# Repeating the pooled-attention means with one fp16 product instead of an fp32 one, with the stage table re-timed

## The chip, the cores and the metric

The kernel runs on one core of a Trainium2 chip. A core has five engines that work side by side, each through its own list of instructions in order: TensorE (PE, matrix products into PSUM), VectorE (DVE), ScalarE (ACT), GpSimd (POOL) and SyncE (SP, which here only issues DMAs). They wait for each other by semaphores. The metric is device time in microseconds (us), and lower is better.

## The reference

The reference is an attention block whose output goes through a mixture of experts. Only the first part is touched here. B = 8 batches, H = 8 heads, S = 576 tokens, D = 64:

```python
q_d = q.reshape(B, H, Sd, factor, D).mean(axis=3)
k_d = k.reshape(B, H, Sd, factor, D).mean(axis=3)
v_d = v.reshape(B, H, Sd, factor, D).mean(axis=3)
out_d = sm_attn(q_d, k_d, v_d)
out_up = np.repeat(out_d, factor, axis=2)
mask = np.abs(pos[:, None] - pos[None, :]) < factor
scores = np.where(mask, scale * np.matmul(q, k.transpose(0, 1, 3, 2)), -1000000000.0)
...
return (out_up + out_local).astype(np.float32)
```

`sm_attn` is softmax attention, here among 144 means of four tokens each; each mean's result then stands for its 4 tokens. `out_local` is softmax attention of each token over the 7 tokens around it.

The sum, laid out as 4608 tokens by 512 values (x), is then routed: gate scores x @ w_gate, a greedy assignment with a capacity of 576 tokens per expert, and for each of 8 experts relu(x @ w1) @ w2 on its own tokens.

## The kernel before

The work has three stages, one after the other. Attention makes x and the gate scores; routing picks an expert and its tokens; the experts' products follow, with later routing beside them.

Attention walks over 36 **units** of 128 tokens (4 windows of 32), 4.5 units to a batch. Batch work (transposing q and k, summing groups of four, attention among the 144 means) is spread between the units. A unit's steps on PE are: `loc_s` (scores, L485 and L494), `loc_t` (four transposes, L514), `loc_v` (32 small products, L536), `rows` (L475, repeats the means), `log_t` (four transposes of x, L554), `log_m` (gate products, L569 and L572). Between them stand, on DVE, the maximum and subtraction after `loc_s` (L503, L504), the `norm` after each half of `loc_v` (L439, L440, L442), the addition of the repeated means (`log_a`, L544), and the low half of x (L559); and, on ACT, the exponential (L506), the copies of the transposed scores (`pt`, L525) and the high half of x (L558).

A batch's means come from `down_v` (L398, L403, L411). Its `end()` normalizes them into `u32`, fp32, 128 means by 512, with DVE. The last 16 of the 144 means, the tail, are spread by POOL into `ut32` (L429). `rows(u)` then makes 128 token rows out of 32 rows of means with a product whose weights `rep` are zeros and ones; a unit that runs over the end of a batch's first 128 means uses two products of 64 rows, one of them with `rept` and `ut32`. This holds for the first 27 units, those of batches 0 to 5 (`ADDU`); for the last nine the means go through DRAM (`UPB` = 6).

The order is written by hand. `run` gives each step a time in units: unit number plus the step's entry in `LOC`, or a place in a spread (`TW`, `DW`) for batch work, or an entry in `NEXT` for a load; it sorts the steps by that time and records them in that order, and each engine runs its own instructions in the order recorded. Steps that use PE are **pieces**; `after(n, f)` records f only n pieces later, and `need(key)` records it at once. `FN`, `FL`, `FT`, `FD` are such distances. `EV` is a cycle that says which copies out of PSUM go to DVE (1) and which to ACT (0). Products write to PSUM tiles named g, of which there are six (`NG`), and one tile named s for the scores.

```python
LOC = {'up': 1.7, 'um': 4.3, 'st': 4.6, 't': 1.3, 'lm': 8.07, 's0': 0.33, 's1': 0.331, 'lt': 5.61, 'v0': 1.83, 'v1': 1.831, 'add': 4.5}
```

Of the kernel before, what the change touches and what calls it, by code (L numbers as in the profile page):

```python
# [6 lines left out]
F32 = mybir.dt.float32  # L7
# [26 lines left out]
GSN = ()  # L34
SH1 = 0.6
EARLY = 1
# [3 lines left out]
LT = 5  # L40
NEXT = (("q0", 1.3), ("q1", 1.6), ("k0", 1.9), ("k1", 2.2), ("t", 2.6), ("q2", 2.9), ("q3", 3.2), ("k2", 3.5), ("k3", 3.8),
        ("v0", 4.1), ("v1", 4.4), ("v2", 4.7), ("v3", 5.0), ("w", 5.2))
VWS = 0.25
PACE0 = 0.6
FD = 4
FN = 2
FL = 3
FT = 2
PEL = ("s0", "s1", "t", "v0", "v1", "lt", "lm")
TW = (0.23, 2.44)  # L50
DW = (0.15, 1.9)
DWS = {0: (1.96, 3.4), 7: (0.82, 2.25)}
LOC = {'up': 1.7, 'um': 4.3, 'st': 4.6, 't': 1.3, 'lm': 8.07, 's0': 0.33, 's1': 0.331, 'lt': 5.61, 'v0': 1.83, 'v1': 1.831, 'add': 4.5}
GS1 = ''
# [8 lines left out]
PEV = (0,0)  # L63
EV = (0,0,0,0,0,1)
UPB = 6
# [4 lines left out]
GS = 32.0  # L70
VWT = 1.75
T0 = (-0.12, 0.19)
LD0 = (-1.79, -1.53, -1.57, -0.7, 0.51)
LD1 = (-0.99, -0.95, -0.9, -0.89, -0.88, -0.6, -0.55, -0.3, -0.25, 0.2, 0.4, 0.6, 0.8, 2.0)
TWS = {1: (1.4, 2.75)}
E0 = 0.54
E1 = 0.55
# [17 lines left out]
class Attention:  # L95
    def __init__(self, ctx, tc, q, k, v, wg, ident, identb, maskc, x_dram, up_dram, lg, big, more=()):
# [14 lines left out]
        self.ident, ident = ident  # L111
        identh = cst.tile([128, 130 + H + GT + QW], BF, name="identb")
        self.identb, self.half, self.own8 = identh[:, :128], identh[:, 128:130], identh[:, 130:130 + H]
        self.own16, self.eye = identh[:, 130 + H:130 + H + GT], identh[:, 130 + H + GT:]
        self.wm = cst.tile([128, 128], BF, name="wm")
# [10 lines left out]
        for i in range(2):  # L126
# [5 lines left out]
            self.vd.append(cst.tile([128, 2, H, D + 1], F32, name=f"vd{i}"))  # L132
        self.rep = cst.tile([128, 4 * 128], F32, name="rep")
        self.rept = cst.tile([128, 4 * GT], F32, name="rept")
        self.u32 = [cst.tile([128, H, D], F32, name=f"u32{i}") for i in range(2)]
        self.ut32 = [cst.tile([128, H, D], F32, name=f"ut32{i}") for i in range(2)]
        for i in range(4):
# [12 lines left out]
    def fixed(self, part):  # L150
# [17 lines left out]
        else:  # L168
# [4 lines left out]
            for t in self.vw[2:]:  # L173
                nc.gpsimd.memset(t, 1.0)
            nc.scalar.copy(self.rep.rearrange("p (g f) -> p g f", f=4), self.identb[:, :, None].to_broadcast([128, 128, 4]))
            nc.scalar.copy(self.rept.rearrange("p (g f) -> p g f", f=4), self.own16[:, :, None].to_broadcast([128, GT, 4]))
            heads(nc.gpsimd, nc.gpsimd, self.qdz[1])
# [213 lines left out]
    def down_v(self, b, g):  # L391
# [21 lines left out]
        def end():  # L413
            x = self.u32[b % 2][:, 4 * g:4 * g + 4]
            r = self.norm(o, x, 4 + g, 4.0)
            if b >= UPB:
                up = self.up_dram[b * G:b * G + 128, 256 * g:256 * g + 256]
                nc.sync.dma_start(up, x.rearrange("p h d -> p (h d)"))
            if g:
                own = self.wk.tile([128, 2], F32, name="own")  # L420
                nc.vector.tensor_tensor(own, r[:, 4:].to_broadcast([128, 2]), self.half, op=OP.mult)
                y = self.wk.tile([128, D], F32, name="yu")
                nc.vector.tensor_scalar(y, o[:, 260:324], own[:, :1], None, op0=OP.mult)
                nc.vector.scalar_tensor_tensor(y, o[:, 325:389], own[:, 1:], y, op0=OP.mult, op1=OP.add)
                if b >= UPB:
                    nc.sync.dma_start(bass.AP(tensor=up.tensor, offset=up.offset - 256 * g + 128 * HD,
                                              ap=[[D, H], [HD, 16], [1, D]]), y)
                else:
                    nc.gpsimd.tensor_tensor(self.ut32[b % 2], y[:, None].to_broadcast([128, H, D]),  # L429
                                            self.own8[:, :, None].to_broadcast([128, H, D]), op=OP.mult)  # L430

        self.after(FN, end, ("v", b, g))

    def norm(self, o, dst, m, n):
# [8 lines left out]
        return r  # L443

    def load_up(self, u):
        for b in {4 * u // NW, (4 * u + 3) // NW}:
            for g in range(2):
                self.need(("v", b, g))
        if u < ADDU:
# [10 lines left out]
    def rows(self, u):  # L460
# [6 lines left out]
        for r0 in (0, 64):  # L467
            b, l = divmod(32 * u + r0 // 4, G)
            t = (self.u32 if l < 128 else self.ut32)[b % 2].rearrange("p h d -> p (h d)")
            parts.append((r0, 64, self.rep[:, 4 * l:4 * l + 64] if l < 128 else self.rept, t, (b, l < 128), l))  # L470
        if parts[0][4] == parts[1][4]:
            l = parts[0][5]
            parts = [(0, 128, self.rep[:, 4 * l:4 * l + 128], parts[0][3])]
        for r0, n, w, t, *_ in parts:
            nc.tensor.matmul(o[r0:r0 + n], w, t, start=True, stop=True)  # L475
        self.up[u] = o
# [880 lines left out]
def _constants():  # L1357
# [11 lines left out]
    for (_, step), (n, nxt) in zip(LV, LV[1:] + ((1, 0),)):  # L1369
# [7 lines left out]
        "ident": np.eye(128, dtype=np.float32),  # L1377
        "identb": np.concatenate([np.eye(128), p[:, None] // 16 % 2 == np.arange(2), p[:, None] // GT == np.arange(H), p[:, None] % GT == np.arange(GT), p[:, None] % 64 == np.arange(QW)], 1).astype(np.float32).astype(bf),
        "mask": m.transpose(2, 0, 1, 3).reshape(128, 4, 4 * KW).astype(bf),
# [29 lines left out]
```

## Time and profile before

| what | value |
|---|---|
| time, median of 3 runs | 741.86 us (738.19 to 743.55) |
| profiled execution, its own time | 735.96 us |
| span of that execution, first to last instruction | 734.1 us |
| busy, whole span: PE / DVE / ACT / POOL | 91% / 72% / 45% / 31% |
| mean granted TensorE clock | 0.964 |

The profile is of one execution, which took 5.9 us less than the median of the three runs. Times in it count from the start of the span. Attention fills some 40 us of start, a steady part from 40 to 240 us, and its last units until about 275 us; the first routing follows until 305 us, and the experts the rest.

### The profile page before, as it was taken

How to read it: one execution, taken by the hardware profiler on the slowest of the kernel's cores; microseconds unless marked ns; L12 is line 12 of the kernel's file. 1: busy time of each engine (PE TensorE's matmuls, PEld its weight loads, DVE VectorE, ACT ScalarE, POOL GpSimd, SP SyncE). 2: the span in 40 equal slices, each digit the busy share in tenths (PEclk: the TensorE clock that was granted, in tenths of full speed). 3: DMA queues.
4: the chain of work that ended last, by engine and by line, in shares of the span. 5: the costliest groups of instructions: out<-in, count | busy, mean ns of one | idle time of the engine just before them, and what ended most of it. 6: DMA issues, size and time to landing. Idle time of an engine off the chain costs nothing.

```text
span 734.1 us, 21924 instructions
## 1 busy us (share of the span) xinstructions
PE 671.5 (91%) x8919; PEld 454.4 (62%) x8919; DVE 527.0 (72%) x1575; ACT 334.0 (45%) x637; POOL 227.3 (31%) x296
## 2 busy tenths in 40 slices
PE   7889998999999872699999899999999999999994
PEld 4677777677777661475575375475575574664751
DVE  5687686778777887897889698798797796534500
ACT  4566657586776430451542443443444334434410
POOL 4766172625626440300601501302204104401011
PEclk9799999999999985799999999999999999999998
DMA  9998959788896650712706706717627439905001
GB/s 267 219 201 225 232 135 244 204 194 202 200 225 171 153 173 12 239 57 93 266 2 232 171 23 255 162 28 267 138 85 242 98 141 234 343 2 122 9 29 37
DMA packets 142356, 116.21 MB, mean 158 GB/s; under 512 B 91440, under 2 KB 120112, under 8 KB 142256
## 3 DMA queue, kind: packets, MB, share of 16 engines
q1 hardware_dynamic: 134960, 93.27, 47.8%
q0 software_dynamic: 6432, 20.98, 9.0%
q8 instruction: 71, 1.16, 0.7%
q10 hardware_dynamic: 864, 0.56, 0.3%
q14 instruction: 29, 0.24, 0.1%
HBM read 88.23 MB, written 19.46 MB: 147 GB/s over the span
## 4 chain that ended last, share of the span: by engine, by line
PE 52%; DVE 17%; issue 15%; ACT 6%; DMA 6%; POOL 2%; SPq 0%; POOLq 0%; ACTq 0%; DVEq 0%
PE pX L1243 13%; PE pH L1202 12%; PE g L536 5%; PE g L475 3%; PE g L318 3%; DVE wl L1126 2%; PE s L494 2%; PE g L554 2%; PE g L514 2%; PE pR L799 2%; DVE ht L1229 2%; DVE level L766 2%; DMA nat<-in_moe_w_dram 1%; POOL out_dram L1253 1%; PE g L398 1%
## 5 line engine op out<-in xcount | busy, mean ns | idle before, releaser
L1202 PE MATMUL pH<-xt,wh 128*128 128x256 f16 (+1 forms) x1024 | 194.7, 286 | 1.6 <-DVE xt L1163 0.8
L1243 PE MATMUL pX<-wh,ht 128*128 128x512 f16 (+1 forms) x640 | 177.9, 380 | 0.0
L1202 PE MATMUL pH<-xt,wl 128*128 128x320 f16 (+1 forms) x512 | 146.2, 286 | 0.0
L1243 PEld LDWEIGHTS <-ht 128*128 128x128 f16 (+1 forms) x960 | 82.1, 100 | 94.6 <-issue 5.4
L1243 PE MATMUL pX<-wl,ht 128*128 128x512 f16 (+1 forms) x320 | 117.6, 380 | 0.0
L1202 PEld LDWEIGHTS <-wh 128*128 128x128 f16 x1024 | 98.0, 98 | 29.3 <-issue 6.3
L1126 DVE SCALAR_TENSOR_TENSOR wl<-nat,wh 128x512 f16<-128x512 f32 x128 | 83.5, 687 | 25.0 <-ACT wh L1124 22.0
L1253 POOL DMA_INDIRECT out_dram<-y,idx x40 | 43.4, 1086 | 181.9 <-ACT y L1250 158.9
L1226 ACT ACTIVATE ht<-pH 128x512 f16<-128x512 f32 (+1 forms) x128 | 45.5, 407 | 114.7 <-PE pH L1202 114.7
L1250 ACT ACTIVATE y<-pX 128x512 f32<-128x512 f32 (+1 forms) x40 | 23.8, 595 | 108.9 <-PE pX L1243 61.4
L1124 ACT ACTIVATE wh<-nat 128x1024 f16<-128x1024 f32 x64 | 67.4, 1053 | 8.7 <-DMA nat<-in_moe_w_dram 8.7
L1229 DVE SCALAR_TENSOR_TENSOR ht<-pH,ht 128x512 f16<-128x512 f32 (+1 forms) x128 | 52.3, 450 | 26.2 <-ACT ht L1226 25.7
L1141 POOL DMA_INDIRECT xg<-x_dram,idx x40 | 42.9, 1071 | 64.8 <-DVE cl L1026 45.5
L1202 PEld LDWEIGHTS <-wl 128*128 128x128 f16 x512 | 50.0, 98 | 13.5 <-issue 1.7
L525 ACT COPY pt<-g 64x512 f32<-64x512 f32 x72 | 41.7, 579 | 33.3 <-PE g L514 31.8
L536 PE MATMUL g<-vw,pt 128*64 128x65 f32 x1152 | 45.9, 230 | 2.7 <-ACT pt L525 2.4
L536 PEld LDWEIGHTS g<-vw,pt 128*64 128x64 f32 x1152 | 40.5, 143 | 9.7 <-ACT pt L525 6.0
L304 ACT COPY qt<-g 64x512 f32<-64x512 f32 (+1 forms) x50 | 31.4, 628 | 32.4 <-PE g L318 19.1
L318 PE MATMUL g<-ident,nat 128*128 128x128 f32 x256 | 41.1, 286 | 3.8 <-DMA nat<-in_q_dram 2.3
L304 ACT COPY kt<-g 64x512 f32<-64x512 f32 (+1 forms) x60 | 37.9, 631 | 9.2 <-PE g L318 8.5
L291 POOL TENSOR_TENSOR gtmp<-kt 128x576 f32<-128x576 f32 x14 | 16.0, 1146 | 78.6 <-ACT kt L304 68.3
L949 POOL MEMSET f<- 128x1 bf16 x8 | 0.9, 109 | 118.7 <-DVE s L888 52.8
(219 smaller groups left out, 1143.7 us busy)
## 6 DMA issues: line engine op xcount, KB each, us to landing
nat<-in_moe_w_dram SPq DMA_DIRECT2D x28, 1024.0 KB
vw<-in_v_dram SPq DMA_DIRECT2D x136, 96.0 KB
x_dram<-x SPq DMA_DIRECT2D x36, 256.0 KB
nat<-in_q_dram SPq DMA_DIRECT2D x32, 256.0 KB
nat<-in_k_dram SPq DMA_DIRECT2D x32, 256.0 KB
nat<-in_v_dram SPq DMA_DIRECT2D x28, 256.0 KB
up<-up_dram SPq DMA_DIRECT2D x9, 256.0 KB
nat<-in_moe_w_dram SPq DMA_DIRECT2D x4, 512.0 KB
```

The source lines that it names most:

```text
L304: self.nc.scalar.copy(out, in_)
L318: nc.tensor.transpose(p[:, a, :, fp], src[:, 4 * hh + 2 * a + s, 2 * fp:2 * fp + 2].rearrange("p f d -> p (f d)"), self.ident)
L525: self.nc.scalar.copy(out, in_)
L536: nc.tensor.matmul(o[64 * i:64 * i + 64, 65 * h:65 * h + 65], pt[:, 2 * (h % 2) + i, 2 * g + h // 2].rearrange("p b q -> p (b q)"), self.v ...
L1124: nc.scalar.activation(hi, r, AF.Copy, scale=sc)
L1126: nc.vector.scalar_tensor_tensor(lo[:, a:a + LOP], r[:, a:a + LOP], sc, hi[:, a:a + LOP], op0=OP.mult, op1=OP.subtract)
L1141: self.fetched = nc.gpsimd.indirect_dma_start(out=xg[:n], out_offset=None, in_=self.x, in_offset=bass.IndirectOffsetOnAxis(ap=idx[:n, c:c ...
L1202: mm = nc.tensor.matmul(p[:, s, :s1 - s0], w[d][a][:, 128 * f:128 * f + 128], xt[:, b, d, s0:s1], start=j == 0, stop=j == len(seq) - 1)
L1226: last = nc.scalar.activation(hi, q, AF.Relu)
L1229: low = nc.vector.scalar_tensor_tensor(lo, q, 0.0, hi, op0=OP.max, op1=OP.subtract)
L1243: mm = nc.tensor.matmul(p[o:o + m], ht[:, f, h0:h0 + m], w[4 + f // 2][b][:, 512 * (f % 2):512 * (f % 2) + 512], start=j < parts, stop=j > ...
L1253: i = nc.gpsimd.indirect_dma_start(out=self.out, in_=y[:n], in_offset=None, out_offset=bass.IndirectOffsetOnAxis(ap=idx[:n, c:c + 1], axis=0))
```

## The change

The normalized means are kept as a pair of fp16 numbers, high and low, each scaled by 32 (`XS`). For means 0 to 63 the high half lies on partitions 0 to 63 and the low half on 64 to 127 of `u16[:, 0]`; for means 64 to 127, `u16[:, 1]` has the high half on 64 to 127 and the low one on 0 to 63. A product over 128 partitions with weights that are 1/32 in row j and row j + 64 then adds the two halves and repeats the mean. `rep` is fp16 and covers 64 means; `rept` is fp16. A unit whose 32 means cross from the first 64 to the next uses two products of 64 rows; a tail uses two products, one with the high and one with the low half.

`end()` writes its fp32 result to a work tile `xu`; `highs` makes the high halves on ACT (four of 64x256 and one of 128x64 for a batch), and `lows`, recorded `FH` pieces later, the low halves on DVE, and spreads the tail on POOL twice. `load_up` sees to it that all is recorded before the first unit that needs it. Batches 6 and 7 keep the way through DRAM. The table of times is also changed: `rows`, `loc_t`, `loc_v`, `log_t`, loads of the next batch, loads of v, distances in pieces, and one copy in five instead of six goes to DVE.

```diff
-SH1 = 0.6
+SH1 = 0.4
-NEXT = (("q0", 1.3), ("q1", 1.6), ("k0", 1.9), ("k1", 2.2), ("t", 2.6), ("q2", 2.9), ("q3", 3.2), ("k2", 3.5), ("k3", 3.8),
-        ("v0", 4.1), ("v1", 4.4), ("v2", 4.7), ("v3", 5.0), ("w", 5.2))
-VWS = 0.25
+NEXT = (("q0", 1.46), ("q1", 1.76), ("k0", 2.06), ("k1", 2.37), ("t", 2.77), ("q2", 3.07), ("q3", 3.38), ("k2", 3.68), ("k3", 3.98),
+        ("v0", 4.28), ("v1", 4.59), ("v2", 4.89), ("v3", 5.19), ("w", 5.4))
+VWS = 0.26
-FN = 2
+FN = 1
+FH = 2
-FT = 2
+FT = 3
-LOC = {'up': 1.7, 'um': 4.3, 'st': 4.6, 't': 1.3, 'lm': 8.07, 's0': 0.33, 's1': 0.331, 'lt': 5.61, 'v0': 1.83, 'v1': 1.831, 'add': 4.5}
+LOC = {'up': 2.07, 'um': 4.35, 'st': 4.6, 't': 1.194, 'lm': 8.07, 's0': 0.33, 's1': 0.331, 'lt': 5.483, 'v0': 1.842, 'v1': 1.843, 'add': 4.5}
-EV = (0,0,0,0,0,1)
+EV = (0, 0, 0, 0, 1)
-VWT = 1.75
+VWT = 1.24
-E0 = 0.54
+E0 = 0.72
...
-        self.rep = cst.tile([128, 4 * 128], F32, name="rep")
-        self.rept = cst.tile([128, 4 * GT], F32, name="rept")
-        self.u32 = [cst.tile([128, H, D], F32, name=f"u32{i}") for i in range(2)]
-        self.ut32 = [cst.tile([128, H, D], F32, name=f"ut32{i}") for i in range(2)]
+        self.rep = cst.tile([128, 4 * 64], F16, name="rep")
+        self.rept = cst.tile([128, 4 * GT], F16, name="rept")
+        self.u16 = [cst.tile([128, 2, H, D], F16, name=f"u16{i}") for i in range(2)]
+        self.ut16 = [cst.tile([128, 2, H, D], F16, name=f"ut16{i}") for i in range(2)]
...
-            x = self.u32[b % 2][:, 4 * g:4 * g + 4]
+            x = self.wk.tile([128, 4, D], F32, name="xu")
...
-                else:
-                    nc.gpsimd.tensor_tensor(self.ut32[b % 2], y[:, None].to_broadcast([128, H, D]),
-                                            self.own8[:, :, None].to_broadcast([128, H, D]), op=OP.mult)
+            if b < UPB:
+                self.after(FH, lambda: self.highs(b, g, x, y), ("h", b, g))
...
+    def highs(self, b, g, x, y):
+
+        nc = self.nc
+        us = []
+        for i in range(2):
+            hi, lo = slice(64 * i, 64 * i + 64), slice(64 - 64 * i, 128 - 64 * i)
+            u16 = self.u16[b % 2][:, i, 4 * g:4 * g + 4]
+            us.append((u16[lo], x[hi], u16[hi]))
+        if g:
+            yh = self.wk.tile([128, 2, D], F16, name="yh", bufs=1)
+            us.append((yh[:, 1], y, yh[:, 0]))
+        for lo, x, hi in us:
+            nc.scalar.activation(hi, x, AF.Copy, scale=XS)
+
+        def lows():
+            for lo, x, hi in us:
+                nc.vector.scalar_tensor_tensor(lo, x, XS, hi, op0=OP.mult, op1=OP.subtract)
+            if g:
+                for i in range(2):
+                    nc.gpsimd.tensor_tensor(self.ut16[b % 2][:, i], yh[:, i, None].to_broadcast([128, H, D]),
+                                            self.own8[:, :, None].to_broadcast([128, H, D]), op=OP.mult)
+
+        self.after(FH, lows, ("l", b, g))
...
-            t = (self.u32 if l < 128 else self.ut32)[b % 2].rearrange("p h d -> p (h d)")
-            parts.append((r0, 64, self.rep[:, 4 * l:4 * l + 64] if l < 128 else self.rept, t, (b, l < 128), l))
+            if l < GM:
+                t, w = (self.u16[b % 2][:, l // 64],), self.rep[:, 4 * (l % 64):4 * (l % 64) + 64]
+            else:
+                t, w = (self.ut16[b % 2][:, 0], self.ut16[b % 2][:, 1]), self.rept
+            parts.append((r0, 64, w, t, (b, l // 64), l))
...
-        for r0, n, w, t, *_ in parts:
-            nc.tensor.matmul(o[r0:r0 + n], w, t, start=True, stop=True)
+        for r0, n, w, ts, *_ in parts:
+            for i, t in enumerate(ts):
+                nc.tensor.matmul(o[r0:r0 + n], w, t.rearrange("p h d -> p (h d)"), start=i == 0, stop=i == len(ts) - 1)
```

The change moves instructions on three engines. Line numbers of the changed kernel are some 30 higher. First PE, at a unit that repeats means of batch 3: here `rows` (writing g from u and rep) stands between `log_m` (reading xt) and `loc_t` (reading sw) before.

```order
L572 MATMUL g<-wg_118,xt 128x8
L318 MATMUL g<-ident,nat 128x128 x4
L475 MATMUL g<-u_136,rep 128x512
L514 MATMUL g<-ident,sw_144 128x128 x4
L485 LDWEIGHTS identb
```

In the changed kernel the same step stands behind `loc_s` (reading kt and qt) and ahead of `log_t` (reading x) and `loc_v` (reading vw and pt); the rows are of a unit without batch work.

```order
L526 MATMUL s<-kt,qt 32x38 x32
L507 LDWEIGHTS rep
L507 MATMUL g<-u_136,rep 128x512
L586 MATMUL g<-ident,x 128x128 x4
L568 MATMUL g<-vw_142,pt_146 64x65 x16
L601 LDWEIGHTS xt
```

So `rows` now lies between `loc_t` and `loc_v`, and no longer between `loc_s` and `loc_t`. Next DVE behind the `down_v` of batch 4 in the changed kernel: u is the fp16 pair, yh that of the tail, xu the fp32 means, and mx and sw belong to the next unit's scores.

```order
L442 TENSOR_SCALAR den<-g 128x4
L443 RECIPROCAL den<-den 128x4
L445 TENSOR_TENSOR x<-g,den 128x256
L464 SCALAR_TENSOR_TENSOR u_135<-xu,u_135 64x256 x4
L464 SCALAR_TENSOR_TENSOR yh<-yu,yh 128x64
L606 TENSOR_REDUCE lg<-g 128x8
L305 COPY kt<-g 64x2x256 x2
L535 TENSOR_REDUCE mx<-s 128x8
L536 TENSOR_TENSOR sw_143<-s,mx 128x8x38
```

The five low halves have been put ahead of the maximum and subtraction of the next scores. Last ACT in the changed kernel, at the same place.

```order
L538 ACTIVATE sw_144<-sw_144 128x8x38
L307 COPY kt<-g 64x2x256 x2
L460 ACTIVATE u_135<-xu 64x256 x4
L460 ACTIVATE yh<-yu 128x64
L307 COPY qt<-g 64x2x256 x2
L557 COPY pt_146<-g 64x16x32 x2
```

The five high halves stand between copies of the next batch's k and q and ahead of the copies `pt`.

## Rows read from the trace of the kernel before

**Rows 1.** By stretch: length; busy of PE, PEld, DVE, ACT, POOL; clock; DMA share; GB/s.

```profile
40.00:240.00 200.00, 191.03 (x4507) 148.22 (x4503) 151.40 (x434) 135.31 (x268) 101.76 (x148) 0.99 0.83 204
240.00:275.00 35.00, 27.45 (x686) 22.96 (x685) 29.28 (x91) 15.40 (x32) 13.87 (x17) 0.90 0.57 160
275.00:305.00 30.00, 12.71 (x129) 8.35 (x126) 23.76 (x98) 6.08 (x8) 3.99 (x6) 0.54 0.30 95
```

**Rows 2.** Waits in 40 to 240 us: total us, times, longest.

```profile
DVE mx L503 <- PE s L494: 25.1, 22, 2.9
DVE den L439 <- PE g L536: 10.9, 10, 3.0
...
PE g L536 <- ACT pt L525: 1.9, 4, 0.5
```

**Rows 3.** Chain that ended last, 128 to 150 us: start, length, what.

```profile
129.04 0.86 PE g L475 x2
...
131.06 0.77 issue
...
139.16 1.01 PE g L475 x4
```

**Rows 4.** Groups by line and shape, L475.

```profile
L475 PE MATMUL g<-u,rep 128*128 128x512 f32 x42 | 22.0, 605 | 0.0
```

**Rows 5.** Timeline of PE in the experts' stage, fp16 products of 512 columns.

```profile
345.50 0.38 PE L1243 MATMUL pX<-wl,ht 128*128 128x512 f16 x1
345.72 0.59 PE L1243 MATMUL pX<-wh,ht 128*128 128x512 f16 x2
346.15 0.38 PE L1243 MATMUL pX<-wl,ht 128*128 128x512 f16 x1
```

**Rows 6.** Groups by line and shape: operations like the added ones.

```profile
L302 DVE COPY qt<-g 64x512 f32<-64x512 f32 x20 | 13.8, 689 | 5.9 <-PE g L318 5.3 <-PE s L494 0.3 <-ACT ptd L304 0.2
L559 DVE SCALAR_TENSOR_TENSOR xt<-g,xt 128x512 f16<-128x512 f32 x36 | 24.6, 684 | 4.9 <-ACT xt L558 4.9
L1229 DVE SCALAR_TENSOR_TENSOR ht<-pH,ht 128x64 f16<-128x64 f32 x64 | 13.6, 213 | 0.0
L1169 ACT ACTIVATE xs<-xg 128x512 f16<-128x512 f32 x24 | 14.8, 627 | 14.6 <-DMA xg<-x_dram,idx 12.9 <-DVE pi L1037 0.9 <-DVE xs L1170 0.7
L1226 ACT ACTIVATE ht<-pH 128x64 f16<-128x64 f32 x64 | 13.9, 218 | 0.0
L429 POOL TENSOR_TENSOR ut<-yu,identb 128x512 f32<-128x512 f32 x6 | 6.3, 1044 | 16.5 <-DVE den L439 16.5
```

**Rows 7.** Busy time in 5 us stretches, first and last with DVE over 4.5.

```profile
40.00:45.00 5.00, 4.50 (x170) 3.89 (x167) 4.54 (x21) 1.62 (x3) 4.61 (x9) 1.00 1.02 205
...
235.00:240.00 5.00, 4.95 (x145) 4.28 (x144) 4.61 (x13) 2.77 (x6) 4.61 (x7) 1.00 0.98 251
```

**Rows 8.** Timeline of DVE; idle time and its releaser in brackets.

```profile
137.24 0.47 DVE L503 TENSOR_REDUCE mx<-s 128x8 f32<-128x304 f32 x1 [1.34 <-PE s L494]
...
165.61 0.47 DVE L503 TENSOR_REDUCE mx<-s 128x8 f32<-128x304 f32 x1 [0.69 <-PE s L494]
```

**Rows 9.** Timeline of ACT at the same places.

```profile
138.32 0.46 ACT L506 ACTIVATE sw<-sw 128x304 f32<-128x304 f32 x1
...
162.85 1.25 ACT L304 COPY qt<-g 64x512 f32<-64x512 f32 x2 [1.97 <-PE g L318]
164.13 1.26 ACT L304 COPY kt<-g 64x512 f32<-64x512 f32 x2
```

**Rows 10.** Timeline of PE: its longest wait in the steady part.

```profile
83.58 1.36 PE L331 MATMUL g<-ident,natt 128*64 128x128 f32 x14 [1.83 <-issue]
```

**Rows 11.** Busy time in 1 us stretches behind that wait.

```profile
84.00:85.00 1.00, 1.00 (x12) 0.67 (x8) 0.00 (x0) 0.00 (x0) 0.00 (x0) 0.57 1.09 326
85.00:86.00 1.00, 1.00 (x9) 0.67 (x11) 0.00 (x0) 0.97 (x3) 0.00 (x0) 0.50 1.17 272
87.00:88.00 1.00, 1.00 (x17) 0.89 (x14) 0.88 (x5) 0.15 (x1) 0.00 (x0) 0.73 1.11 223
```

More of the change, by code (lines that the diff above doesn't have):

```diff
@@ L111, in __init__ @@
         self.ident, ident = ident
-        identh = cst.tile([128, 130 + H + GT + QW], BF, name="identb")
+        identh = cst.tile([128, 194 + H + GT + QW], BF, name="identb")
         self.identb, self.half, self.own8 = identh[:, :128], identh[:, 128:130], identh[:, 130:130 + H]
-        self.own16, self.eye = identh[:, 130 + H:130 + H + GT], identh[:, 130 + H + GT:]
+        self.own16, self.eye = identh[:, 130 + H:130 + H + GT], identh[:, 130 + H + GT:130 + H + GT + QW]
+        self.own64 = identh[:, 130 + H + GT + QW:]
         self.wm = cst.tile([128, 128], BF, name="wm")
@@ L174, in fixed @@
                 nc.gpsimd.memset(t, 1.0)
-            nc.scalar.copy(self.rep.rearrange("p (g f) -> p g f", f=4), self.identb[:, :, None].to_broadcast([128, 128, 4]))
-            nc.scalar.copy(self.rept.rearrange("p (g f) -> p g f", f=4), self.own16[:, :, None].to_broadcast([128, GT, 4]))
+            for t, i, n in ((self.rep, self.own64, 64), (self.rept, self.own16, GT)):
+                nc.scalar.activation(t.rearrange("p (g f) -> p g f", f=4), i[:, :, None].to_broadcast([128, n, 4]),
+                                     AF.Copy, scale=1.0 / XS)
             heads(nc.gpsimd, nc.gpsimd, self.qdz[1])
@@ L418, in end @@
                 nc.sync.dma_start(up, x.rearrange("p h d -> p (h d)"))
+            y = None
             if g:
@@ L447, in load_up @@
             for g in range(2):
-                self.need(("v", b, g))
+                for n in "vhl":
+                    self.need((n, b, g))
         if u < ADDU:
@@ L468, in rows @@
             b, l = divmod(32 * u + r0 // 4, G)
-            t = (self.u32 if l < 128 else self.ut32)[b % 2].rearrange("p h d -> p (h d)")
-            parts.append((r0, 64, self.rep[:, 4 * l:4 * l + 64] if l < 128 else self.rept, t, (b, l < 128), l))
+            if l < GM:
[3 more added lines that the diff above has]
+            parts.append((r0, 64, w, t, (b, l // 64), l))
         if parts[0][4] == parts[1][4]:
-            l = parts[0][5]
+            l = parts[0][5] % 64
             parts = [(0, 128, self.rep[:, 4 * l:4 * l + 128], parts[0][3])]
-        for r0, n, w, t, *_ in parts:
-            nc.tensor.matmul(o[r0:r0 + n], w, t, start=True, stop=True)
+        for r0, n, w, ts, *_ in parts:
+            for i, t in enumerate(ts):
+                nc.tensor.matmul(o[r0:r0 + n], w, t.rearrange("p h d -> p (h d)"), start=i == 0, stop=i == len(ts) - 1)
         self.up[u] = o
@@ L1377, in _constants @@
         "ident": np.eye(128, dtype=np.float32),
-        "identb": np.concatenate([np.eye(128), p[:, None] // 16 % 2 == np.arange(2), p[:, None] // GT == np.arange(H), p[:, None] % GT == np.arange(GT), p[:, None] % 64 == np.arange(QW)], 1).astype(np.float32).astype(bf),
+        "identb": np.concatenate([np.eye(128), p[:, None] // 16 % 2 == np.arange(2), p[:, None] // GT == np.arange(H), p[:, None] % GT == np.arange(GT), p[:, None] % 64 == np.arange(QW), p[:, None] % 64 == np.arange(64)], 1).astype(np.float32).astype(bf),
         "mask": m.transpose(2, 0, 1, 3).reshape(128, 4, 4 * KW).astype(bf),
```

## Prediction

> **What bounds the kernel now.** I read the busy times by stretch first. From 40 to 240 us PE is busy 191.0 of 200 us, DVE 151.4, ACT 135.3 and POOL 101.8, and the DMA share is 0.83 [rows 1]; in the two stretches behind, DVE is the busiest engine, and the clock falls to 0.54 in the second. So PE bounds the steady part, and every product with `rep` lies in it. The waits say the same from the other side: DVE stands still for PE's scores 25.1 us in 22 places and for `loc_v` 10.9 us in 10, while PE's wait for an ACT copy is 1.9 us in all [rows 2]. The chain that ended last has `rows` in it at each unit, 0.86 us for a full unit and 1.01 for one with a tail [rows 3]. What is taken from PE there shortens the kernel, as long as DVE, the next fullest, follows.
>
> **The change part by part.** *PE's products, removed.* The trace shows each fp32 product of 512 columns as two instructions: 42 for the 21 units with one product of 128 rows [rows 4]. In the chain a full one costs 0.86 us. An fp16 product of 512 columns costs 0.65 / 3 = 0.216 us: in the experts' stage three of them fill the time from 345.50 to 346.15 [rows 5]. After the change 18 units have one fp16 product: 18 x (0.86 - 0.216) = 11.6 us. Three units cross from mean 63 to 64 and have two of 64 rows: between 0.22 us, if they run side by side as the two fp32 halves of a tail did (1.01 us for four instructions that would need 1.72 in a row), and 0.43, one after the other; taken 0.33: 3 x 0.53 = 1.6. Six units with a tail have three products, 0.43 to 0.65 us, taken 0.54: 6 x 0.47 = 2.8. Sum **16.0 us** off PE, bounds 15.0 to 17.
>
> *The halves, added.* Per batch, for six batches, ACT makes four of 64x256 and one of 128x64, DVE the same number. The trace has 512 and 64 columns: on DVE 684 and 213 ns, on ACT 627 and 218 [rows 6]. On the line between them 256 columns cost 0.415 and 0.393 us. DVE: 24 x 0.415 + 6 x 0.213 = 11.2 us; ACT: 24 x 0.393 + 6 x 0.218 = 10.7 us. POOL gets 6 x 1.04 = 6.3 us, on an engine that is half empty; nothing reads its result for more than a unit, so nothing. The new `EV` moves two pairs of copies and one single from ACT to DVE by the recorded order: 4 x 0.689 [rows 6], and 0.4 for half as many columns, = 3.2 us. DVE then has 151.4 + 14.4 = 165.8 us of work in about 184, that is 90%; ACT 142.8, 78%; PE 175, 95%.
>
> *What DVE cannot give.* Two terms. (a) In 7 of the 40 stretches of 5 us DVE is busy over 4.5 us [rows 7]; where it is full, PE's saving turns into waiting: 16.0 x 7 / 40 = 2.8 us, and the same share of the moved copies, 0.6. (b) The five low halves stand ahead of the next scores' maximum: 4 x 0.415 + 0.213 = 1.87 us. At such a place DVE had 0.69 us idle ahead of that maximum (165.61) [rows 8], so the maximum is 1.2 us late. Behind it PE wants the exponential for `loc_t`: maximum at 137.24, exponential ended at 138.78 [rows 8, 9], 1.54 us. PE used to have `log_t`, `loc_v`, `log_m` and `rows` in between, and now has the first three, about 2.1 us: some 0.5 us to spare. So 0.7 us of waiting per batch, 6 x 0.7 = 4.2 us; bounds 0 (ACT's and PE's other work moves with it) and 6 x 1.87 = 11.2 us.
>
> *The order of steps.* `rows` moves from between `loc_s` and `loc_t` to between `loc_t` and `loc_v`. What it costs is in (b); what it gives is time for the copies `pt`, the 1.9 us that PE waited for [rows 2]: -1.9 us, bounds 0 and -1.9. The loads of the next batch come some 0.16 units later and v's windows half a unit later, on SP's queue, which nothing else of the steady part waits behind but the stores of x; the windows are still asked for three units before `loc_v` reads them, and I put this at nothing. The bound on the bad side is the longest wait of PE, at the tail of q and k: 1.83 us [rows 10], after which the clock was 0.50 to 0.57 from 84 to 87 us and rising in the next [rows 11]; it may go (-3.5 with the slow stretch) or stay. `FN` = 1 lets DVE ask for the means a piece earlier; `FT` = 3 holds a g tile a piece longer. Both sit in gaps that DVE has (1.34 us at 137.24 [rows 8]), cost nothing where these are, and are part of (a) where not. `E0` moves steps of the first two units by 0.18 units or less: nothing.
>
> *Sum.* -16.0 + 2.8 + 0.6 + 4.2 - 1.9 = **-10.3 us**. Against the profiled execution's 735.96 us this is 725.7; that execution was 5.9 us under the median, so on the median's footing 741.86 - 10.3 = **731.6 us**.
>
> **The rivals.** *DVE becomes the bound.* The saving is kept off PE but DVE, at 90%, sets the pace. For it: PE and DVE are both lists in a fixed order, and DVE's idle time is made of small waits for PE, not of one gap. With (b) at its upper bound of 11.2 and all 3.2 us of copies on the path, -16.0 + 2.8 + 11.2 + 3.2 = +1.2, and with half of that -16.0 + 2.8 + 5.6 + 1.6 - 1.9 = -7.9: from 734 to 743, middle 738. Against it: the stretches behind `down_v` are among DVE's emptier ones (0.69 and 1.34 us idle in each unit [rows 8]). There is no row in the steady part of a DVE operation that reads two SBUF tensors while POOL works, as the low halves do; POOL is busy for half the time there, so if they stood still whenever it works, DVE would have 11.2 x 0.51 = 5.7 us more. At (b)'s rate of 0.7 / 1.87 that is 2.1 us on the path, 733.7, and in full 737.3: inside this rival. The Trainium skill, in the GPSIMD Engine Reference, under Specifications, says that GpSimd's SBUF interfaces are shared with VectorE and that instructions with two SBUF inputs contend for them; no run here shows it yet, and by it this rival is likelier.
>
> *All of it fits.* DVE's waits shrink and PE's do not grow: -16.0 - 1.9, and the 1.83 us wait and its slow clock gone too (-3.5): 720 to 726, middle 724. For it: 36 us of DVE's idle time are waits for PE [rows 2]. Against it: the seven full stretches.
>
> *Slower: the halves block both lists.* The high halves stand behind copies of the next batch's k on ACT. At the place of `down_v` ACT ran two pairs of copies from 162.85 to 165.39 [rows 9], just behind the batch's last products of that kind. DVE would stand at the first low half until ACT comes to the high ones, 1.3 us and more, with the next scores behind it; and ACT's copies `pt` stand behind 1.8 us of high halves. If PE then waits 1.83 us twice per batch, and its clock falls once as it did at 84 us (the rows from 84 to 88 us, with 0.50 between the last two shown, lose 0.43 + 0.50 + 0.50 + 0.27 = 1.7 us [rows 11]), that is 5.4 us per batch and 32 in all: 741.9 - 16 + 32 = **758 us**. It decides at waits of PE near 1.8 us: the trace's 0.77 us wait at 131.06 [rows 3] was not followed by a slower clock. Against it: ACT had 1.97 us idle just before those copies [rows 9], and the high halves of the first 256 columns could be made there.
>
> **How the numbers follow.** Chances: forecast 0.48 (725 to 736), DVE as the bound 0.25, all fits 0.17, slower 0.10. 1% is 7.4 us, about what a measurement of this kernel can tell from no change: faster is below 734.4. Of the forecast 0.38 lies below and 0.10 above; of DVE as the bound 0.03 below; all of the third: faster 0.58. Slower over 1% takes most of the last case: 0.09. The same 0.33. The range reaches from the middle of the third case to the end of the second: **724 to 743 us**.
>
> **What would show it.** Right: the group of products with `rep` at 18 + 6 instructions of 0.21 us spacing; the steady part some 10 us shorter, with PE still over 93% busy and DVE near 90%; DVE's waits for the scores well under 25 us; PE's waits for the exponential at `loc_t` near 4 us, in the unit behind each `down_v`; no wait for `pt`. (b) is wrong if these units show no wait, or one over 1 us. The second case shows as waits of PE for DVE or for g tiles all along the steady part, or as low halves much over 0.42 us; the slower one as granted clocks of 0.5 in the steady part, once per batch. The forecast also fails if the loads, at a DMA share that rises from 0.83 to about 0.9, come late for the transposes: PE would then wait at L318 or L331 of the old numbering.

## The result, and the profile after

| | median | range | runs |
|---|---|---|---|
| before | 741.62 us | 738.19 to 743.55 | 4 |
| after | 730.58 us | 727.65 to 734.29 | 4 |

The recorded ratio is 0.9887 (95%: 0.984 to 0.9933): the change makes the kernel 1.1% faster, some 8 us. It is not the ratio of the two medians, which lie 11.0 us apart. The execution that was profiled is the slowest of the four, 734.29 us with a mean granted clock of 0.945; the other three had 0.955 to 0.964. It serves to find places; what a part is worth comes from the timed comparisons below. All the lines named from here on are those of the changed kernel, some 32 higher than before (L475 is now L507, `mx` L535, `loc_t` L546, `loc_v` L568).

The steady part in the windows of the kernel after (columns as in [rows 1]):

```profile
40.00:240.00 200.00, 181.29 (x4575) 149.06 (x4570) 169.95 (x472) 143.52 (x295) 109.39 (x155) 0.95 0.82 203
```

PE's busy time in the steady part fell from 191.0 to 181.3 us and DVE's rose from 151.4 to 170.0. But PE now stands still for 18.7 of 200 us instead of 9.0, and its clock is 0.95 instead of 0.99 there. Had PE alone set the pace, its idle time would not have doubled: the saving has met other limits.

The waits of the kernel after, 40 to 240 us (total, times, longest):

```profile
DVE mx L535 <- PE s L526: 7.5, 9, 2.0
...
PE g L546 <- ACT sw L538: 6.0, 5, 2.7
...
PE s L526 <- issue: 3.4, 4, 1.8
...
PE g L321 <- issue: 2.4, 1, 2.4
```

DVE's wait for the scores fell from 25.1 us [rows 2] to 7.5. In its place PE waits 6.0 us for the exponential `sw` at `loc_t`, which is the wait that the prediction named, and for what it didn't name: "issue", where the profile shows no releaser.

The new operations, by source line (duration min, median, max in ns; first and last start):

```profile
L507 PE MATMUL g<-u,rep x30: 389/396/634, 57.6 to 229.9; 128*128 128x512 f16 x18, 128*64 128x512 f16 x12
L507 PE MATMUL g<-ut,rept x12: 379/403/637, 80.1 to 230.1; 128*64 128x512 f16 x12
...
L464 DVE SCALAR_TENSOR_TENSOR u<-xu,u x24: 418/420/1387, 45.0 to 193.5; 64x256 f16<-64x256 f32 x24
L464 DVE SCALAR_TENSOR_TENSOR yh<-yu,yh x6: 226/226/365, 48.6 to 194.0; 128x64 f16<-128x64 f32 x6
...
L460 ACT ACTIVATE u<-xu x24: 401/414/423, 42.1 to 190.4; 64x256 f16<-64x256 f32 x24
L460 ACT ACTIVATE yh<-yu x6: 256/256/257, 44.3 to 190.9; 128x64 f16<-128x64 f32 x6
```

Number and size of the additions are as forecast (0.42 us against 0.415 on DVE, 0.41 against 0.393 on ACT). The exception is the maximum of 1.39 us among the low halves, to which the chain and the timelines below come back.

The chain of the kernel after at its longest wait for the exponential (start, length, what):

```profile
68.09 0.42 DVE u L464
...
68.53 0.42 DVE u L464
...
68.96 0.69 DVE qt L305
...
69.67 0.69 DVE qt L305
...
70.39 0.42 DVE u L464
...
70.84 0.42 DVE u L464
...
71.29 0.23 DVE yh L464
...
71.55 0.49 DVE mx L535
72.06 0.49 DVE sw L536
72.56 0.47 ACT sw L538
...
73.08 1.11 PE g L546 x4
```

Read it from below: PE's transposes wait for ACT's exponential, that for DVE's subtraction and maximum, and the maximum stands in DVE's list behind five low halves and two copies of q, 3.4 us of work that none of the scores needs. The two copies are there by the new `EV`. PE stood still for 2.70 us, and the windows of 1 us behind it show the clock go to 0.50, the lower of its two levels (1.2 instead of 2.4 GHz), for some six microseconds in which PE is busy all the time:

```profile
72.00:73.00 1.00, 0.00 (x0) 0.00 (x0) 0.97 (x3) 0.43 (x1) 1.00 (x2) 0.69 0.34 42
73.00:74.00 1.00, 0.92 (x4) 0.71 (x4) 0.97 (x4) 0.02 (x1) 0.92 (x2) 0.50 0.81 232
...
79.00:80.00 1.00, 1.00 (x74) 0.77 (x73) 1.00 (x2) 0.46 (x1) 0.92 (x2) 0.90 0.58 139
```

### The profile page after: what moved, and what is told of

It reads as the page before. It is cut to its first block, busy times and chain, and to the rows that moved or that the text cites. A ratio compares the mean times of both kernels' runs of the same rounds, so it can differ in the third digit from the quotient of the medians.

```text
span 732.6 us, 21918 instructions
## 1 busy us (share of the span) xinstructions
PE 661.4 (90%) x8895; PEld 454.4 (62%) x8895; DVE 542.8 (74%) x1610; ACT 341.1 (47%) x662; POOL 232.3 (32%) x302
## 4 chain that ended last, share of the span: by engine, by line
PE 49%; DVE 21%; issue 15%; ACT 6%; DMA 4%; POOL 2%; SPq 1%; ACTq 0%; POOLq 0%; DVEq 0%
PE pX L1275 15%; PE pH L1234 13%; PE g L568 3%; PE g L321 2%; PE g L546 2%; DVE wl L1158 2%; PE s L526 2%; DVE ht L1261 2%; PE pR L831 2%; DVE level L798 2%; POOL out_dram L1285 1%; PE g L401 1%; PE g L586 1%; DMA vw<-in_v_dram 1%; ACT kt L307 1%
## 5 line engine op out<-in xcount | busy, mean ns | idle before, releaser
L1234 PEld LDWEIGHTS <-wl 128*128 128x128 f16 x512 | 50.2, 98 | 13.3 <-issue 1.2
L568 PE MATMUL g<-vw,pt 128*64 128x65 f32 x1152 | 47.2, 235 | 5.7 <-ACT kt L307 2.0
L568 PEld LDWEIGHTS g<-vw,pt 128*64 128x64 f32 x1152 | 41.7, 147 | 12.3 <-issue 4.6
L321 PE MATMUL g<-ident,nat 128*128 128x128 f32 x256 | 41.8, 288 | 6.7 <-DMA nat<-in_q_dram 2.9
L294 POOL TENSOR_TENSOR gtmp<-kt 128x576 f32<-128x576 f32 x14 | 16.1, 1150 | 70.9 <-ACT kt L307 47.2
L321 PEld LDWEIGHTS g<-ident,nat 128*128 128x128 f32 x256 | 29.7, 145 | 12.3 <-DMA nat<-in_q_dram 4.0
```

What stands on the lines that cost most here:

```text
L321: nc.tensor.transpose(p[:, a, :, fp], src[:, 4 * hh + 2 * a + s, 2 * fp:2 * fp + 2].rearrange("p f d -> p (f d)"), self.ident)
L568: nc.tensor.matmul(o[64 * i:64 * i + 64, 65 * h:65 * h + 65], pt[:, 2 * (h % 2) + i, 2 * g + h // 2].rearrange("p b q -> p (b q)"), self.v ...
L1234: mm = nc.tensor.matmul(p[:, s, :s1 - s0], w[d][a][:, 128 * f:128 * f + 128], xt[:, b, d, s0:s1], start=j == 0, stop=j == len(seq) - 1)
```

## The experiments

The theory to be tested was the prediction's: the shorter product takes 16 us from PE, most of it arrives at the end, DVE's low halves give back some 4, and the table of times is worth little. Its rivals: the table does it alone; DVE's work eats the saving. Each ratio is to the kernel before, timed in the same series on one chip (three series, with medians of 737.41, 738.01 and 736.24 us for it). To put a ratio into microseconds its distance from 1 is multiplied by 738.

### Table and code apart

`after_again` is the changed kernel once more, with more runs. 

> The changed kernel once more, for a second profile. Both theories: 730.6 us, give or take 2, 11 us under the kernel before. If the spread of its runs (727.7 to 734.3) comes from stretches in which PE waited and its clock fell, a faster execution than the profiled one (734.3) shows a higher mean clock than 0.945 and fewer 5 us stretches under 1.00.

Measured: 730.03 us, ratio 0.9915 (0.9884 to 0.9945), -6.3 us. The first result's -8.3 lies near the other end of the same interval; from here on this ratio is the one that is compared. The profiled execution, 727.74 us, had a mean clock of 0.961 instead of 0.945, and 5 of the 40 stretches of 5 us below 1.00 instead of 8, as expected.

`table_only` gives the old code the new numbers, `code_only` the new code the old ones:

```diff
 table_only: old code
-SH1, NEXT, VWS, FN, FT, LOC, EV, VWT, E0 as before
+SH1, NEXT, VWS, FN, FT, LOC, EV, VWT, E0 as after
 code_only: new code
-SH1, NEXT, VWS, FN, FT, LOC, EV, VWT, E0 as after
+SH1, NEXT, VWS, FN, FT, LOC, EV, VWT, E0 as before
```

> The kernel before with the changed kernel's table of times, and nothing else: the means stay fp32. Theory 1 (the gain is PE time saved by the fp16 products, 16 us less what DVE takes back): 738 to 746, no gain. Theory 2 (the gain comes from the new order and distances, the product is a side matter): 728 to 735.

> The fp16 halves and products with the old table of times. Theory 1: PE's 16 us are saved here too, and the old order leaves PE more work between the scores and the transposes of them, so 727 to 735, with waits for the copies pt as before. Theory 2: 738 to 745.

Measured: `table_only` 725.54 us, 0.986 (0.9825 to 0.9895), -10.3 us; `code_only` 744.33 us, 1.0092 (1.0063 to 1.0122), +6.8 us. The first is 2.5 us below Theory 2's range, the second inside it. That is the finding of this case. The table alone, on the old fp32 product, gives more than the whole change, and the fp16 product with its halves makes the kernel slower with either table: by 6.8 us on the old one, and by 4.1 on the new (0.9915 against 0.986), give or take 3.4, since the two intervals overlap a little.

In this order: the windows of `table_only`, its longest waits of PE, and the longest wait of PE in `code_only` (total, times, longest):

```profile
40.00:240.00 200.00, 195.44 (x4735) 153.85 (x4743) 163.46 (x462) 136.15 (x275) 103.81 (x149) 1.00 0.85 209
```

```profile
PE s L494 <- issue: 1.7, 4, 0.5
PE g L382 <- ACT sd L366: 1.2, 2, 0.9
```

```profile
PE g L568 <- ACT pt L557: 8.8, 7, 2.2
```

In `table_only` PE stands still for 4.6 of 200 us instead of 9.0, the waits for `pt` [rows 2] are gone, and so are the 1.83 us at 83.58 [rows 10] and the slow clock behind them [rows 11]: the clock is 1.00. That is 4.4 us of idle time and some 2 of clock, most of the 8.3 us by which its last repeat starts earlier (223.0 us against 231.3). These are single executions: in the profile of `loads_only` below the 1.83 us wait and its slow clock are gone too, and that kernel is 0.7 us faster and no more. In `code_only`, where `rows` stands ahead of `loc_t` as before, the 1.9 us of waiting for `pt` have become 8.8; with `rows` behind `loc_t`, in the changed kernel, they are 0.3, and 1.4 in `after_again`. That fits the link that the prediction saw (`rows` covers the copies), but the two kernels differ in the whole table, and `um_only`, next, moves `rows` alone. Whether ACT's high halves or PE's shorter list made the wait longer in `code_only` was not separated.

### Which part of the table

```diff
 loc_only: old code, and of the table only
+LOC = {'up': 2.07, 'um': 4.35, ..., 't': 1.194, ..., 'lt': 5.483, 'v0': 1.842, 'v1': 1.843, ...}
+E0 = 0.72
 loads_only
+SH1, NEXT, VWS, VWT as after
 rest_only
+FN = 1; FT = 3; EV = (0, 0, 0, 0, 1)
 um_only: old code, one entry: rows behind loc_t and the next scores
-LOC = {... 'um': 4.3 ...}
+LOC = {... 'um': 4.35 ...}
```

> The kernel before with the new places of PE's steps alone (LOC, E0): fp32 means, old loads, old distances, old EV. Theory A (the place of the repeating product between the transposes of the scores and the product that reads them is what the new table gives: it covers ACT's copies pt): 8 to 12 us under the kernel before. Theory B (the loads): within 3 us. Theory C (distances and EV, copies moved from ACT to DVE): within 3 us.

> The kernel before with the new times of the loads alone (SH1, NEXT, VWS, VWT). Theory A: within 3 us of the kernel before. Theory B (windows of v asked for later leave the queues to q and k, and PE's longest wait and its slow clock go): 5 to 12 us under. Theory C: within 3 us.

> The kernel before with FN = 1, FT = 3 and one copy in five on DVE, nothing else. Theory A: within 3 us of the kernel before, or slower by up to 3. Theory B: the same. Theory C: 5 to 12 us under.

> The kernel before with one number changed: rows at 4.35 instead of 4.3, which puts the fp32 product behind the scores in each unit and moves nothing else. If its place covering ACT's copies pt is what the new places gave (9.4 us): 6 to 10 us under the kernel before. If it is the other entries (the transposes and products against the batch's own steps): within 3 us.

Measured:

| kernel | us | ratio (95%) | x 738 |
|---|---|---|---|
| loc_only | 730.12 | 0.9873 (0.9836 to 0.9909) | -9.4 |
| loads_only | 736.98 | 0.9991 (0.9965 to 1.0016) | -0.7 |
| rest_only | 734.85 | 0.9957 (0.993 to 0.9983) | -3.2 |
| um_only | 734.5 | 0.9963 (0.9934 to 0.9993) | -2.7 |

The loads give nothing that can be measured, as predicted. The three parts sum to -13.3, against -10.3 together, so they share some of their gain. Moving `rows` alone is worth 2.7 us, give or take 2.2; `LOC` and `E0` as a whole are worth over three times that. The 2.7 is near the 1.9 forecast, but not for the reason given: in the profile of `um_only` PE still waits 1.5 us for `pt`, against 1.9 before, while `loc_only` has no such wait in its list. So `loc_only` met the time that its Theory A gave, and the place of `rows` is not what met it. The rest lies in the other entries (`t`, `lt`, `v0`, `v1`, `up`, and `E0`) or in their working together with it; they move `loc_t`, `log_t` and `loc_v` by 0.01 to 0.13 units against the batch's steps, and `up`'s load. Which of them it is was not taken apart.

### What the low halves cost

`no_lows` leaves the low halves out (they are zeros, written once at the start, so the means keep only their fp16 high half):

```diff
-            for lo, x, hi in us:
-                nc.vector.scalar_tensor_tensor(lo, x, XS, hi, op0=OP.mult, op1=OP.subtract)
...
+            nc.gpsimd.memset(self.yh[:, 1], 0.0)
+            for t in self.u16:
+                nc.gpsimd.memset(t[64:, 0], 0.0)
+                nc.gpsimd.memset(t[:64, 1], 0.0)
```

> The changed kernel without the low halves of the means: they are zeros written once, so the repeated means have only their high fp16 halves. DVE has 11 us less. Theory 1 (DVE gives back part of the saving, mostly through the low halves ahead of the scores): 4 to 9 us under the changed kernel, 721 to 727, and PE's waits for the exponential fall from 6 us to under 2. Rival (DVE's fullness does not matter, PE's own work sets the pace): within 1.5 us of the changed kernel, 729 to 732.

Measured: 721.62 us, 0.9808 (0.9777 to 0.9839). Against 0.9915 with them, the low halves on DVE cost 7.9 us, as Theory 1 had it. Its sign came half: PE's waits for the exponential fell to 3.0 us, none over 0.8, and not to under 2.

`pool_lows` computes them, on POOL, from means that are already normalized to the scale of 32; `pool_all` has the high halves there too:

```diff
 pool_lows
-            r = self.norm(o, x, 4 + g, 4.0)
+            r = self.norm(o, x, 4 + g, 4.0 if b >= UPB else 4.0 / XS)
-            nc.scalar.activation(hi, x, AF.Copy, scale=XS)
+            nc.scalar.activation(hi, x, AF.Copy, scale=1.0)
-                nc.vector.scalar_tensor_tensor(lo, x, XS, hi, op0=OP.mult, op1=OP.subtract)
+                nc.gpsimd.tensor_tensor(lo, x, hi, op=OP.subtract)
 pool_all, besides
-            nc.scalar.activation(hi, x, AF.Copy, scale=1.0)
+            nc.gpsimd.tensor_copy(hi, x)
```

> The changed kernel with the low halves made by POOL instead of DVE (the means are scaled by 32 when they are normalized, so that a plain subtraction does; all of the result is computed). If DVE's 11 us of low halves are what costs (8.4 us without them): 5 to 9 us under the changed kernel, 721 to 725. If POOL delivers them late, or DVE suffers from POOL's work: 727 or more, with waits of PE for POOL at the repeating product.

> The same with the high halves on POOL too, so that neither DVE nor ACT does any of the halves' work. If the halves as a whole cost 14 us (the changed kernel with four-fold products against the table alone) and PE's shorter product gives 10: 715 to 721, below the kernel before, the changed one and the table alone (725.5). If POOL becomes late or the place on ACT was free: 722 or more.

Measured: 723.33 us, 0.9809 (0.9774 to 0.9844), and 723.14 us, 0.9798 (0.9759 to 0.9837). With the whole computation done, `pool_lows` is as fast as the kernel that leaves it out, so the cost was not the arithmetic but its place on DVE. Taking the high halves off ACT as well gives nothing that can be measured (0.9798 against 0.9809); PE then waits 1.4 us once for POOL's `u` at the product, so that their place on ACT was free is likely and not shown. Both kernels beat the one before by 1.9 and 2.0% and the changed one; against `table_only` the intervals overlap, at some 4 us.

Of `pool_lows`: the windows, its longest waits of PE, and the low halves by source line:

```profile
40.00:240.00 200.00, 185.16 (x4840) 152.02 (x4843) 166.47 (x474) 149.57 (x309) 129.32 (x188) 1.00 0.89 212
```

```profile
PE s L526 <- issue: 3.8, 5, 1.3
PE g L546 <- ACT sw L538: 3.3, 7, 0.8
```

```profile
L464 POOL TENSOR_TENSOR u<-xu,u x24: 662/668/683, 50.4 to 183.7; 64x256 f16<-64x256 f32 x24
```

A low half takes longer on POOL, 0.67 against 0.42 us, and PE and DVE never wait for it. No wait for the exponential is over 0.8 us now, none of the listed waits is over 1.3, and the clock is 1.00. But PE still stands still for 14.8 of 200 us, three times as long as in `table_only`, whose product takes nearly four times as long. Added up over both kernels' lists, PE waits 6.7 us for "issue" instead of 2.3 and 3.3 for the exponential instead of 0.2.

`lows_behind` keeps the low halves on DVE but records them behind the next scores' maximum and subtraction:

```diff
-        self.after(FH, lows, ("l", b, g))
+        self.low_due.append(lows)
 in loc_s, behind the subtraction
+        while self.low_due:
+            self.low_due.pop(0)()
```

> The changed kernel with the low halves on DVE recorded behind the next scores' maximum and subtraction instead of ahead of them. If their place costs (they delay the exponential that the transposes of the scores wait for): 3 to 7 us under the changed kernel, 723 to 727, and the waits of PE for the exponential fall from 6 us to under 2. If it is their amount on a full DVE: within 2 us of the changed kernel.

Measured: 738.82 us, 1.0019 (0.9993 to 1.0045), 7.7 us slower than `after_again`. The theory that the place just ahead of the maximum is the harm, and a later one would heal it, fell. The source line of the low halves in `lows_behind` shows one thing that went wrong:

```profile
L464 DVE SCALAR_TENSOR_TENSOR u<-xu,u x24: 418/469/1258, 43.4 to 197.1; 64x256 f16<-64x256 f32 x24
L464 DVE SCALAR_TENSOR_TENSOR yh<-yu,yh x6: 224/310/1059, 50.6 to 198.4; 128x64 f16<-128x64 f32 x6
```

The median rose from 420 to 469 and from 226 to 310 ns, and together they take 19.2 us instead of 14.0 in `after_again`: 22 of the 30 now overlap an operation of POOL, where it was 10. They also stand ahead of DVE's other work in a unit, the additions to x among it (PE waits 2.3 us once for `xt`), and PE's wait for the exponential is still 4.1 us instead of under 2. PE's waits for "issue" are 7.7 us, one of them 2.8. Which of these makes up the 7.7 us was not separated.

### How much of PE's saving arrives

`rows_4x` is the changed kernel with each repeating fp16 product done four times:

```diff
-        for r0, n, w, ts, *_ in parts:
-            for i, t in enumerate(ts):
+            for _ in range(4):
+                for i, t in enumerate(ts):
```

> The changed kernel with every fp16 product that repeats means done four times over, the same values each time, so that PE spends about as long on them as on the fp32 ones (0.86 us in a full unit). Theory 1 (PE's saved 16 us reach the end): 12 to 16 us slower than the changed kernel, 742 to 746. The rival, after the table alone gave 12 us (under the new table PE waits for DVE and ACT, and a product placed there is covered): within 4 us, 729 to 734, and a granted clock in the steady part nearer to 1.00 than 0.96.

Measured: 739.76 us, 1.0023 (0.9996 to 1.0051), between the ranges of the two theories, with the clock at 0.97 in the steady part. First a full unit's products in its chain (start, length, what), then the windows narrowed to the line of the products, 40 to 240 us, in `rows_4x` and in `after_again` (busy time of PE and of its weight loads, clock, DMA share, GB/s):

```profile
103.89 0.98 PE g L508 x4
```

```profile
40.00:240.00 200.00, 35.95 (x168) 12.59 (x168) 0.97 0.78 197
40.00:240.00 200.00, 12.60 (x42) 2.94 (x42) 0.97 0.84 205
```

Four fp16 products are longer than the fp32 one they were to stand for: 0.98 us against 0.86 [rows 3], and a tail's twelve 1.86 against 1.01. The run therefore serves for its slope, not as a kernel of equal PE time. Between it and `after_again` PE is busy 36.0 and 12.6 us with these products, 23.4 us apart, and the times are 8.0 us apart (1.0023 against 0.9915), give or take 3. So a third of the work that was added here arrives (a fifth to a half, by the intervals). That the same share of a saving arrives is an inference from it.

## Why the prediction came out where it did

The forecast time, 731.6 us, was met to 1.0 us by the first median, and most of the reasons were not right. That was luck. Three terms were wrong, and they cancel in part; and the forecast started from 741.86 us, where the three series put the kernel before at 736 to 738. Of the saving of 10.3 us, `after_again` shows 6.3:

| term | forecast | measured | from |
|---|---|---|---|
| order of steps and rest of the table | -1.9 | -10.3 | table_only |
| shorter product, what arrives | -16.0 + 2.8 + 0.6 = -12.6 | -3.8 | pool_lows against table_only |
| low halves on DVE | +4.2 | +7.8 | after_again against pool_lows |
| sum | -10.3 | -6.3 | after_again |

The middle row holds the high halves on ACT and POOL's part too, and its two ratios come from different series; with intervals of 0.7% each it is -3.8 give or take 4. `rows_4x` points the same way: a third of 16 is 5.3. The rows add up because each is the difference of two ratios.

**What PE's products take: right.** 18 full products, and 12 and 12 of 64 rows (the sign "18 + 6" left out the six with `rep` in the units with a tail; the sum had them). In the timeline of `pool_lows` a full one starts at 68.06 and the next product at 68.29, 0.23 us (forecast 0.216), and a tail takes 0.56 (forecast 0.54):

```profile
68.06 0.39 PE L507 MATMUL g<-u,rep 128*128 128x512 f16 x1
68.29 0.60 PE L586 MATMUL g<-ident,x 128*128 128x128 f32 x4
...
72.11 0.40 PE L507 MATMUL g<-ut,rept 128*64 128x512 f16 x1
...
72.36 0.38 PE L507 MATMUL g<-ut,rept 128*64 128x512 f16 x1
72.67 0.55 PE L586 MATMUL g<-ident,x 128*128 128x128 f32 x3
```

PE's busy time at the product's line says the same: 28.4 us in the kernel before, 12.6 in `after_again`. So the 16.0 us are gone from PE. That they are gone from the path is the step that failed.

**(a), the share that DVE cannot give: the failed step.** It took 7 of 40 stretches in which DVE is busy over 4.5 us, and so lost 2.8 us of 16. The measured loss is some 11 to 12 us. The counting assumed that wherever DVE has room, PE's list moves up freely. `pool_lows` shows the opposite: a clock of 1.00, DVE at 166.5 of 200 us, and PE still loses its saving in waits of 1.3 us and less, for its own "issue", for the exponential and for ACT's copies. It stands still 10.2 us longer than in `table_only`; 4.4 of them are "issue" and 3.1 the exponential. The prediction's own signs, PE over 93% busy and DVE near 90%, came out at 91% and 85% in the kernel after. A unit is a round trip (scores, maximum, subtraction, exponential, transposes, copies, products), and the long fp32 product was work that PE could do while the other engines made theirs. PE's 95% in [rows 1] was a sign that its list was well covered, not only that it was the bound. That the cover is what was lost is how these lists read; the runs show the loss and the waits, not each link, and no run takes one of these waits away alone.

**(b), the low halves: right in kind, half the size.** The wait is where it was put: PE for the exponential at `loc_t`, 6.0 us in 5 places (forecast 4.2 in 6). Moving them to POOL brings it to 3.3, none over 0.8, and the time down by 7.8 us; so about half of that wait is theirs, and most of their cost lies elsewhere. By the trace three things were left out of the 4.2. The moved copies of q fall into the same row and make 1.87 us into 3.4. A wait that long brings the slow clock, which the rival "slower" priced: one such stretch from 73 to 79 us loses about 3 us by itself, and in all the clock is 0.95 to 0.97 in the steady part of the changed kernel against 1.00 in `table_only` and `pool_lows`. And in batch 0 the low halves themselves took twice their time, next.

**The rival "DVE becomes the bound".** Its worked-out limit (low halves standing still while POOL works) happens, but in batch 0 alone, and once more for one low half of batch 4 (0.81 us). The timelines of DVE and POOL of the kernel after, batch 0 and batch 2:

```profile
45.02 3.57 DVE L464 SCALAR_TENSOR_TENSOR u<-xu,u 64x256 f16<-64x256 f32 x4
48.62 0.36 DVE L464 SCALAR_TENSOR_TENSOR yh<-yu,yh 128x64 f16<-128x64 f32 x1
...
49.30 0.42 DVE L445 TENSOR_TENSOR x<-g,den 128x256 f32<-128x256 f32 x1
...
102.33 1.77 DVE L464 SCALAR_TENSOR_TENSOR u<-xu,u 64x256 f16<-64x256 f32 x4
```

```profile
45.03 0.99 POOL L267 TENSOR_TENSOR vd<-gtv 128x256 f32<-128x256 f32 x1
46.10 1.34 POOL L266 TENSOR_TENSOR gtv<-nat 128x512 f32<-128x512 f32 x1
47.52 0.78 POOL L267 TENSOR_TENSOR vd<-gtv 128x256 f32<-128x256 f32 x1
...
104.50 1.04 POOL L467 TENSOR_TENSOR ut<-yh,identb 128x512 f16<-128x512 f16 x1 [2.05 <-DVE lg L606]
```

Beside POOL's sums the four low halves take 3.57 us; at 102.33, with POOL idle from 102.45 to 104.50, 1.77. The Trainium skill, in the GPSIMD Engine Reference, under Specifications, says that GpSimd's SBUF interfaces are shared with VectorE and that VectorE instructions with two SBUF inputs contend for them. The trace agrees, with 3.57 us against 1.77. It costs 1.8 us on DVE in batch 0; behind it PE waits 2.44 us at 49.83 ("issue" at L321) and 1.44 at 55.15 (for DVE's `sd`).

```profile
49.83 0.63 PE L321 MATMUL g<-ident,nat 128*128 128x128 f32 x4 [2.44 <-issue]
```

The first wait is one for DVE, though the profile names no releaser. PE starts 0.10 us after DVE's `x` at L445 has ended, the first operation behind the low halves that is done with a g tile; `after_again`, `code_only` and `rows_4x` have the same wait, and it ends 0.10 us after that operation in each. In the lists of `no_lows` and `pool_lows` the first wait is missing and the second is missing or 0.2 us. Moving POOL's sums away from there was not tried.

**The order of steps: the right sign, a fifth of the size.** The wait for `pt` went (1.9 us to none in the list of `table_only`, 0.3 and 1.4 in the changed kernel), but `um_only` shows that moving `rows` is neither what took it away nor what gave the 10.3 us. The prediction has no term for the new times of `loc_t`, `log_t` and `loc_v` and put `E0` at nothing; `loc_only`, which has these, gives 9.4 us, with the share of each left open. PE's idle time of 9.0 us in 200 and its clock of 0.99 put about 11 us within the reach of a better order, and the prediction listed 1.9 of them.

**The rival "slower".** Its mechanism was there: in the kernel after, the waits of 1.44 us (55.15, six microseconds behind the one of 2.44), of 2.70 (73.08), of 1.97 (132.95, for ACT's copies of k), of 2.13 (167.56, for the exponential) and of 1.85 (194.25, "issue") were each followed by stretches at a granted clock of 0.50, while in `pool_lows`, with none over 1.3 in PE's list, the clock is 1.00. Its point of decision, 1.8 us, is not sharp: behind the same wait of 1.44 us in `after_again` (53.94) the clock stayed at 1.00. The slow clock came at five places in six batches, near the once per batch of its sign, and at two in `after_again`; but such waits did not come twice in each batch, so its 758 us were far off. **"All of it fits"** (724) is about where `pool_lows` lies, and for another reason: the table.

## What to carry to other kernels

When a change brings a new order of steps with it, time that order on the old arithmetic first: here it alone was worth 10 us, and the whole change 6 to 8. Work taken from the fullest engine shortens the kernel only as far as the round trips around it have slack, and here that was about a third, though the engine was 95% busy. New operations belong on the engine that nobody waits for, even if each takes longer there (0.67 us on POOL instead of 0.42 on DVE, and 8 us faster), and VectorE operations with two SBUF inputs not beside GpSimd's work (here 0.42 us alone and up to 1.39 beside it).

## What the runs showed of the hardware that was not expected

PE's "issue" waits come at a fixed count of instructions. In `pool_all` PE's timeline has such waits inside runs of equal products:

```profile
152.09 0.32 PE L414 MATMUL g<-vd,ptd 128*32 128x65 f32 x7 [0.56 <-issue]
...
156.66 0.27 PE L526 MATMUL s<-kt,qt 64*32 64x38 f32 x6 [0.76 <-issue]
...
161.62 0.22 PE L526 MATMUL s<-kt,qt 64*32 64x38 f32 x1 [1.31 <-issue]
```

and the windows between them hold these numbers of products and weight loads:

```profile
152.09:156.66 4.57, 3.81 (x125) 3.35 (x126) 3.80 (x15) 2.53 (x5) 4.05 (x10) 1.00 0.76 183
156.66:161.62 4.96, 3.65 (x127) 3.00 (x126) 4.18 (x12) 2.22 (x4) 4.74 (x7) 1.00 0.93 256
```

With those that PE's sequencer keeps to itself (a window counts an instruction that crosses its edge) it is 256 from each such wait to the next, here and at 185.19 to 190.15. The kernel before has them at the same distance (126.3, 131.83, 136.94 us), and its longest wait, the 1.83 us at 83.58 [rows 10], is one of them. In the fourteen profiles, from 40 to 240 us, 78 of PE's 83 "issue" waits of 0.2 us and more lie on this grid of 256; four of the other five are the wait for DVE in batch 0. The list of DMA queues of the kernel before has a queue of instructions (packets, MB, share of 16 engines):

```profile
q8 instruction: 71, 1.16, 0.7%
```

That is 16 KB a packet, and PE's trace has 18146 instructions, 70.9 times 256. In the traces each of the 78 waits ends 1.1 to 1.7 us after such a packet has landed. So these are waits for the next block of PE's own instructions. Why a packet comes in time for one block and 1.31 us late for another, no run here shows. The waits are not set by the length of PE's list alone: with the fp32 product they are 1.6 to 5.6 us (most in `loc_only`), with the single fp16 one 3.4 to 9.0, and with the fourfold one 0.6. `pool_lows` has 6.7 and `table_only` 2.3, so a part of the saving that did not arrive went here.
